# Where softmax row sums lie in DRAM: one attention kernel, two layouts

## Chip, cores and metric

The kernel runs on one core of a Trainium2 chip. The metric is the device time of one execution in microseconds (us); for several runs the median is given. The engines are named as in the profile: PE (TensorE, matmuls), PEld (its weight loads), DVE (VectorE), ACT (ScalarE), POOL (GpSimd), SP (SyncE, which here only issues transfers; its queue is SPq).

## What is computed

A transformer block with conditioning: attention over a window of a key and value cache, then a gated MLP. Cut to the part that the change touches (32 query heads on 16 key/value heads, 2048 queries, a window of 512 keys, head size 128):

```python
q = (x @ wq).reshape(B, Sq, Hq, Dh).transpose(0, 2, 1, 3)
k = jnp.repeat(k_cache[:, :, Sk - W:, :], rep, axis=1)
v = jnp.repeat(v_cache[:, :, Sk - W:, :], rep, axis=1)
scores = jnp.einsum("bhqd,bhkd->bhqk", q, k) * (Dh ** -0.5)
p = softmax(scores, axis=-1)
o = jnp.einsum("bhqk,bhkd->bhqd", p, v)
return o.transpose(0, 2, 1, 3).reshape(B, Sq, Hq * Dh) @ wo
```

Before it come a layer norm with shift and gain, and behind it a gate and the sum with x; then a second layer norm, `silu(h @ w1) * (h @ w3) @ w2`, a gate and a sum.

## The kernel before

The 2048 queries are cut into 4 blocks of SB = 512, and each block into ST = 4 tiles of P = 128. One head of one block is a slot; there are n = 128 slots, in an order written out by hand. f32 operands are split into a high and a low f16 part, so that a product is three matmuls.

Slot i has four steps, t = 0 to 3. In each, PE makes the scores of one tile (L395), DVE takes their maximum (L399, L400), and ACT takes the exponential p (L412) with the sum of each row beside it, in column t of a small tile l of 128 partitions. The work of neighbouring slots is laid between. Of slot i - 1, p is transposed by PE (L435), copied as the high part by ACT (L436), and DVE subtracts for the low part (L458); for one tile of four a DMA transpose on SPq does it (L451). At the end of slot i PE forms the unnormalized output po of slot i - 1, which has head dimension by queries (L468).

The sums of the rows lie one query per partition, but po has its queries along the free dimension. So they are turned by way of DRAM, in `sums` (slot i - 1, called in slot i): at step 0 the reciprocal of the four sums of each partition (L419), at step 1 the store of 128 x 4 values into a DRAM tile row (L422), and at step 2 the load of those 512 values into every partition, as tile r (L425). Both transfers are issued by SP, whose queue takes all other loads and stores of the stage in order too; L425 waits there until the data of L422 have landed, and L451 follows behind it.

In slot i, step 2, between the maximum of the third tile and the exponential of it, DVE multiplies po of slot i - 2 by r (`normalize`, L477) to give on. At step 3 `split_on` makes its high part on ACT (L487) and its low part on POOL (L488), and later PE multiplies with wo (L348) and DVE adds into acc (L496).

Row is stored as it lies in l: partition p, then t. Query t * 128 + p of the block is thus at place 4p + t of r, and L477 walks through r with `r.rearrange("d p t -> d t p")`.

From slot 16 on the same stage also makes the operands of the MLP ready: loads of w1, w3 and w2 (the tiles wraw and w2raw), sums and splits (wmade and omade), and stores of them (wd and od). The MLP itself (L757, L843) begins near the end of the attention stage; there DVE also has sums and products of the form f32 from PSUM with f32 from SBUF (L938, L944). L310 transposes keys; hp at L446 is the input of the DMA transpose. The load of the conditioning vector c into the tile sc at the very start (L98) takes its values one by one from DRAM, four to a partition.

Of the kernel before, what the change touches and what calls it, by code (L numbers as in the profile page):

```python
# [9 lines left out]
F32 = mybir.dt.float32  # L10
# [9 lines left out]
P = 128  # L20
# [4 lines left out]
SB = 512  # L25
NSB = S // SB
ST = SB // P
# [19 lines left out]
def tile_block(  # L47
# [14 lines left out]
    nc = tc.nc  # L62
# [4 lines left out]
    pool = ctx.enter_context(tc.tile_pool(name="pool", bufs=2))  # L67
    odd = ctx.enter_context(tc.tile_pool(name="odd", bufs=2))
    psum = ctx.enter_context(tc.tile_pool(name="psum", bufs=2, space=PSUM))
    dram = ctx.enter_context(tc.tile_pool(name="dram", bufs=1, space=DRAM))  # L70
# [344 lines left out]
    def sums(i, step):  # L415

        st = state[i]
        if step == 0:
            nc.vector.reciprocal(st["l"][:, ST:], st["l"][:, :ST])  # L419
        elif step == 1:  # L420
            st["row"] = dram.tile([P, ST], F32, name=f"row{i}")
            nc.sync.dma_start(st["row"], st["l"][:, ST:])  # L422
        elif step == 2:
            st["r"] = pool.tile([P, P, ST], F32, tag="kv", name="r", bufs=8)
            nc.sync.dma_start(  # L425
                st["r"].rearrange("d p t -> d (p t)"), st["row"].rearrange("p t -> (p t)").partition_broadcast(P)
            )

    def turn(i, t):

# [42 lines left out]
    def normalize(i):  # L473
        st = state[i]
        po = st.pop("po")
        on = st["on"] = pool.tile([P, SB], F32, tag="raw", name="on", bufs=RB)
        nc.vector.tensor_mul(  # L477
            on.rearrange("d (t p) -> d t p", t=ST),
            po.rearrange("d (t p) -> d t p", t=ST),
            st["r"].rearrange("d p t -> d t p"),  # L480
        )

    def split_on(i):
        st = state[i]
# [809 lines left out]
    for c in range(3):  # L1294
        i = 117 + 3 * c
# [107 lines left out]
    for i in range(n + 2):  # L1403
        run(i, -1)
        for t in range(ST):
# [9 lines left out]
            if 2 <= i <= n and t == 2:  # L1415
                normalize(i - 2)
# [8 lines left out]
            if 1 <= i <= n and t < 2:  # L1425
                sums(i - 1, t)
# [12 lines left out]
            if 1 <= i <= n and t == 2:  # L1439
                sums(i - 1, t)  # L1440
# [3 lines left out]
        if i == n:  # L1444
            normalize(n - 1)
            split_on(n - 1)
# [30 lines left out]
```

## Time and profile before

| | |
|---|---|
| median of 3 runs | 2908.57 us (2904.57 to 2909.78) |
| the profiled execution | 2906.05 us |
| its span | 2904.1 us |
| granted PE clock, mean | 0.995 |
| instructions | 47894 |
| DMA packets, bytes | 416049, 396.33 MB |

The span is the time from the first to the last instruction in the profile. Busy time of an engine is the time in which it worked on an instruction; matmuls overlap, so a busy PE is not PE at its peak. A wait is put down to the instruction that released it. Of a transfer, the profile gives the time from its issue to its landing.

### The profile page before, as it was taken

The page shows a single profiled execution, that of the slowest core. Times are in us where ns is not written, and L with a number is a line of the kernel's source. Part 1 is how long each engine was busy: PE and PEld are TensorE (multiplying, and loading weights), DVE is VectorE, ACT ScalarE, POOL GpSimd, SP SyncE. Part 2 cuts the span into 40 slices and gives each one's busy share as a digit, 9 for nine tenths or more (in the row PEclk, how much of TensorE's full clock was granted, in tenths as well). Part 3 has the DMA queues.
Part 4 walks back from the last instruction along what each step waited for, and adds up shares of the span by engine and source line. Part 5 has one row for each costly group of instructions (what it writes and reads, how often), then busy time and mean ns, then how long its engine had stood idle before and what let it go on. Part 6 is the DMA issues. An engine that isn't in the chain of part 4 may idle for free.

```text
span 2904.1 us, 47894 instructions
## 1 busy us (share of the span) xinstructions
PE 2832.3 (98%) x16624; PEld 1664.3 (57%) x16624; DVE 2104.7 (72%) x3762; ACT 1603.7 (55%) x3168; POOL 1668.0 (57%) x1796
## 2 busy tenths in 40 slices
PE   6999999999999999999999999999999999999998
PEld 3555556565655565555656555555555555555555
DVE  7777788888888888888786665666666665665656
ACT  4676777777777777787755662333333333323332
POOL 3344787778778777888722543445555455343345
PEclk9999999999999999999999999999999999999999
DMA  5535655665556577776734662444343443333332
GB/s 147 135 94 149 154 148 139 151 149 144 140 136 156 133 157 192 184 196 180 183 77 109 156 182 82 128 131 142 121 133 113 156 125 113 117 113 103 106 107 78
DMA packets 416049, 396.33 MB, mean 136 GB/s; under 512 B 180928, under 2 KB 302912, under 8 KB 415040
## 3 DMA queue, kind: packets, MB, share of 16 engines
q1 hardware_dynamic: 415200, 393.28, 49.8%
q8 instruction: 131, 2.15, 0.3%
q14 instruction: 110, 0.90, 0.1%
q10 hardware_dynamic: 608, 0.00, 0.0%
HBM read 263.60 MB, written 95.99 MB: 124 GB/s over the span
## 4 chain that ended last, share of the span: by engine, by line
PE 49%; DVE 2%; POOL 2%; issue 1%; ACT 1%; DMA 1%; SPq 0%; POOLq 0%; DVEq 0%; ACTq 0%
PE py L757 15%; PE px L757 11%; PE pe L843 6%; PE pf L843 6%; PE pe L348 3%; PE po L468 2%; PE pss L395 2%; PE pq L337 2%; PE pt L435 1%; DVE table L399 0%; PE pq L341 0%; DVE acc L496 0%; POOL omade L701 0%; DMA oraw<-in_A_wo 0%; DVE on L477 0%
## 5 line engine op out<-in xcount | busy, mean ns | idle before, releaser
L412 ACT ACTIVATE p<-pss,table,factors 128x512 f32<-128x512 f32 x512 | 399.0, 779 | 399.8 <-DVE table L400 329.4
L757 PEld LDWEIGHTS <-wset 128*128 128x128 f16 x3528 | 345.4, 98 | 337.0 <-issue 1.1
L757 PE MATMUL py<-hset,wset 128*128 128x512 f16 x2016 | 482.7, 379 | 0.0
L348 PE MATMUL pe<-o 128*128 128x288 f16 x3072 | 460.1, 287 | 5.8 <-DVE acc L496 5.8
L399 DVE TENSOR_REDUCE table<-pss 128x1 f32<-128x512 f32 x512 | 350.0, 684 | 133.9 <-PE pss L395 129.1
L395 PE MATMUL pss<-k,qT 128*128 128x512 f16 x1536 | 418.8, 381 | 2.5 <-ACT p L412 1.2
L348 PEld LDWEIGHTS <-o 128*128 128x128 f16 x3072 | 301.1, 98 | 176.8 <-issue 7.4
L468 PE MATMUL po<-ptw,v 128*128 128x512 f16 x1536 | 357.1, 380 | 6.1 <-DVE on L477 3.7
L757 PE MATMUL px<-hset,wset 128*128 128x512 f16 x1512 | 361.6, 379 | 0.0
L458 DVE TENSOR_TENSOR ptw<-pt,ptw 128x512 f16<-128x512 f32 x384 | 263.0, 685 | 62.3 <-ACT ptw L436 59.6
L93 POOL TENSOR_TENSOR akv<-u,akv 128x512 f16<-128x512 f32 x141 | 164.4, 1175 | 218.1 <-ACT akv L92 216.1
L488 POOL TENSOR_TENSOR o<-on,o 128x512 f16<-128x512 f32 x128 | 148.5, 1160 | 241.7 <-ACT o L487 219.6
L337 PE MATMUL pq<-hT,wq 128*128 128x512 f16 x1092 | 282.7, 381 | 1.6 <-DVE hT L205 1.6
L496 DVE SCALAR_TENSOR_TENSOR acc<-pe,factors,acc 128x576 f32<-128x576 f32 x256 | 208.0, 812 | 96.3 <-PE pe L348 76.4
L436 ACT CAST ptw<-pt 128x512 f16<-128x512 f32 x384 | 224.7, 585 | 69.2 <-PE pt L435 67.6
L435 PE MATMUL pt<-ident,p 128*128 128x128 f32 x1536 | 233.4, 275 | 15.8 <-ACT p L412 9.3
L468 PEld LDWEIGHTS <-v 128*128 128x128 f16 x1536 | 149.3, 99 | 169.0 <-issue 11.2
L843 PEld LDWEIGHTS <-akv 128*128 128x128 f16 x1728 | 169.1, 98 | 89.3 <-issue 0.8
L435 PEld LDWEIGHTS pt<-ident,p 128*128 128x128 f32 x1536 | 187.2, 143 | 52.5 <-ACT p L412 14.3
L662 POOL TENSOR_TENSOR wmade<-wraw,wmade 128x256 f16<-128x256 f32 x252 | 172.4, 684 | 53.7 <-ACT wmade L661 34.4
L395 PEld LDWEIGHTS <-qT 128*128 128x128 f16 x1536 | 150.5, 98 | 78.7 <-DVE qT L385 3.7
L337 PEld LDWEIGHTS <-wq 128*128 128x128 f16 x1104 | 109.0, 99 | 138.2 <-issue 8.3
(224 smaller groups left out, 4871.9 us busy)
## 6 DMA issues: line engine op xcount, KB each, us to landing
wset<-wd SPq DMA_DIRECT2D x213, 320.0 KB, 3.3
wd<-wmade SPq DMA_DIRECT2D x108, 320.0 KB, 3.7
r<-row SPq DMA_DIRECT2D x128, 256.0 KB, 4.2
oset<-od SPq DMA_DIRECT2D x106, 288.0 KB, 2.8
wraw<-in_B_w SPq DMA_DIRECT2D x144, 128.0 KB, 3.5
od<-omade SPq DMA_DIRECT2D x57, 288.0 KB, 3.8
wset<-wd SPq DMA_DIRECT2D x71, 160.0 KB, 2.3
w2raw<-in_B_w SPq DMA_DIRECT2D x38, 288.0 KB, 3.5
```

The source lines that it names most:

```text
L337: nc.tensor.matmul(ps, w[:, k // 2, m, :], hT[:, DC + m if k == 1 else m, :], start=s == 0, stop=False)
L348: nc.tensor.matmul(E[:, h, :HALF], o[:, x, rows], w[:, y, h * HALF : (h + 1) * HALF], start=first and n == 0, stop=last and n == 2,)
L395: nc.tensor.matmul(pss, q[:, x, rows], k[:, y, :], start=n == 0, stop=n == 2)
L399: nc.vector.tensor_reduce(nm[:, 0:1], pss, axis=AX.X, op=ALU.max, negate=True)
L412: nc.scalar.activation(p, pss, AF.Exp, bias=nm[:, 1:2], scale=factor, accum_out=st["l"][:, t : t + 1])
L435: nc.tensor.transpose(ps[:, j, :], p[:, j * P : (j + 1) * P], ident)
L436: nc.scalar.copy(st["pt"][:, 0, :, t * P : (t + 1) * P], st["t"])
L458: nc.vector.tensor_sub(pt[:, 1, :, cols], state[i]["t"], pt[:, 0, :, cols])
L468: nc.tensor.matmul(po, v[:, x, c, :], pt[:, y, c, :], start=c == 0 and n == 0, stop=c == KC - 1 and n == 2)
L496: nc.vector.scalar_tensor_tensor(a, E[:, :, :HALF], factors[:, uses[u][0], 2:3], a, op0=ALU.mult, op1=ALU.add)
L757: nc.tensor.matmul(ps, w[:, a, :], h[:, b, :], start=start and n == 0, stop=stop and n == 6, skip_group_check=True)
L843: nc.tensor.matmul(ps[:, h, :HALF], a[:, rows], w[:, b, :], start=m == 0, stop=m == 2)
```

## The change

The DRAM tile row has the shape 4 x 128 in place of 128 x 4, and the store writes it through a transposed view, so that query t * 128 + p lies at place 128t + p. The load copies 512 contiguous values to each partition as before, and r is a plain tile of 128 x 512. The multiplication takes po and r as they lie.

```diff
         elif step == 1:
-            st["row"] = dram.tile([P, ST], F32, name=f"row{i}")
-            nc.sync.dma_start(st["row"], st["l"][:, ST:])
+            st["row"] = dram.tile([ST, P], F32, name=f"row{i}")
+            nc.sync.dma_start(st["row"].rearrange("t p -> p t"), st["l"][:, ST:])
         elif step == 2:
-            st["r"] = pool.tile([P, P, ST], F32, tag="kv", name="r", bufs=8)
-            nc.sync.dma_start(
-                st["r"].rearrange("d p t -> d (p t)"), st["row"].rearrange("p t -> (p t)").partition_broadcast(P)
-            )
+            st["r"] = pool.tile([P, SB], F32, tag="kv", name="r", bufs=8)
+            nc.sync.dma_start(st["r"], st["row"].rearrange("t p -> (t p)").partition_broadcast(P))
...
         on = st["on"] = pool.tile([P, SB], F32, tag="raw", name="on", bufs=RB)
-        nc.vector.tensor_mul(
-            on.rearrange("d (t p) -> d t p", t=ST),
-            po.rearrange("d (t p) -> d t p", t=ST),
-            st["r"].rearrange("d p t -> d t p"),
-        )
+        nc.vector.tensor_mul(on, po, st["r"])
```

## Prediction

> **What bounds the kernel now.** I read the page first, then the busy times stretch by stretch, because the change touches only the attention stage, whose normalizations run from 85.7 to 1754.9 us.
>
> ```profile
> span 2904.1 us, 47894 instructions
> PE 2832.3 (98%) x16624; PEld 1664.3 (57%) x16624; DVE 2104.7 (72%) x3762; ACT 1603.7 (55%) x3168; POOL 1668.0 (57%) x1796
> ...
> core 0: us, PE busy (x) PEld busy (x) DVE busy (x) ACT busy (x) POOL busy (x), PEclk, DMA share, GB/s
> 60.00:500.00 440.00, 427.43 (x2520) 255.80 (x2518) 351.08 (x721) 311.49 (x633) 253.48 (x296) 0.99 0.53 135
> 500.00:1000.00 500.00, 493.76 (x2970) 297.91 (x2968) 414.17 (x830) 376.20 (x793) 387.09 (x484) 1.00 0.58 144
> 1000.00:1400.00 400.00, 390.79 (x2339) 234.06 (x2338) 340.84 (x691) 305.83 (x639) 329.02 (x398) 1.00 0.71 180
> 1400.00:1500.00 100.00, 96.51 (x583) 58.10 (x582) 75.41 (x159) 59.72 (x129) 47.94 (x54) 0.98 0.54 136
> 1500.00:1740.00 240.00, 237.47 (x1420) 142.59 (x1419) 166.24 (x321) 147.08 (x295) 93.18 (x85) 1.00 0.54 138
> ```
>
> TensorE (PE) is the bound in every stretch. VectorE (DVE), the next one, is at 80 to 85% until 1400 us. From 60 to 1740 us PE is idle for 12.6 + 6.2 + 9.2 + 3.5 + 2.5 = 34 us of 1680. That is the first fence around any gain: work taken from VectorE can only give back the part of these 34 us that VectorE causes. The waits of PE and of its weight loads (PEld) in the stretch 60 to 1740 us say which part that is. Columns: waiting engine and line, what it waited for, us in total, times, longest.
>
> ```profile
> PE pt L435 <- ACT p L412: 9.3, 10, 1.7
> PE po L468 <- DVE on L477: 3.7, 7, 1.2
> PE pt L435 <- DVE ptw L458: 2.8, 4, 0.8
> PE pt L310 <- DVE ptw L458: 1.5, 3, 0.6
> ...
> PEld pt L435 <- ACT p L412: 14.3, 15, 2.1
> PEld L468 <- DVE on L477: 5.5, 9, 1.5
> ```
>
> The instruction that changes, L477, is itself the releaser for 3.7 us on PE. The low parts of the transposed probabilities (L458), which stand behind it on VectorE, account for another 4.3 us.
>
> **The normalization itself.** Its rows, and those of the other products and sums of one operand in PSUM and one in SBUF with 512 columns of f32 out:
>
> ```profile
> L477 DVE TENSOR_TENSOR on<-po,r 128x512 f32<-128x512 f32 x128 | 139.3, 1088 | 2.1 <-PE po L468 1.8 <-issue 0.2
> L938 DVE TENSOR_TENSOR u<-px,u 128x512 f32<-128x512 f32 x72 | 49.8, 692 | 93.2 <-ACT u L937 93.2
> L944 DVE TENSOR_TENSOR u<-px,u 128x512 f32<-128x512 f32 x72 | 49.3, 685 | 0.7 <-PE px L757 0.7
> ```
>
> L477 takes 1088 ns, and the same form with both operands contiguous takes 685 to 692. The only difference that the code shows is the walk through r: element (p, t) lies at 4p + t, so successive elements are 16 bytes apart. After the change r is read in order, so I put the new time at 688 ns. The saving is 400 ns a head block, times 128 = 51.2 us of VectorE (2104.7 to about 2053.5). Most of it falls where PE does not wait and is worth nothing. What counts is where L477 stands just ahead of a release. The last of these places in the timeline:
>
> ```profile
> 1572.83 1.07 DVE L477 TENSOR_TENSOR on<-po,r 128x512 f32<-128x512 f32 x1
> ...
> 1573.83 0.68 DVE L458 TENSOR_TENSOR ptw<-pt,ptw 128x512 f16<-128x512 f32 x1
> ...
> 1574.65 0.63 PE L435 MATMUL pt<-ident,p 128*128 128x128 f32 x4 [0.68 <-DVE ptw L458]
> ```
>
> The low part starts when the normalization ends, and PE stands for 0.68 us until it is done; 0.4 us of that goes. The sum over such places:
> - L468 waiting for L477: 7 times, mean 0.53 us, so 7 x 0.40 = 2.8 us.
> - L435 and L310 waiting for L458: 7 times, 4.3 us. I take 5 of them as standing behind a normalization like the one above: 2.0 us.
> - L435 waiting for p: ScalarE waits there for a maximum that VectorE delivers. L477 lies between the maxima of the third and the fourth tile, so I count about a quarter of PEld's 15 waits: 4 x 0.40 = 1.6 us.
> - The end of the stage has one normalization in an unbroken row of VectorE work that PE waits for, the one of the next fence: 0.4 us.
>
> ```profile
> 1739.15 1.06 DVE L477 TENSOR_TENSOR on<-po,r 128x512 f32<-128x512 f32 x1
> ...
> 1743.42 2.74 PE L348 MATMUL pe<-o 128*128 128x288 f16 x12 [2.28 <-DVE acc L496]
> ```
>
> Together 6.8 us. What is late next in such a slot is PE itself, so I let the gain stand. The upper end of the gain takes PEld's 5.5 us, all 4.3 us and half of the 9.3 us: 14.5 us.
>
> **The store.** L422 wrote 16 bytes from each of 128 partitions in one piece. It now writes four single f32 from each, 512 bytes apart in DRAM: 512 pieces where there were 128. The read L425 stays 128 pieces of 2048 bytes. SyncE's queue (SPq) runs in order: L425 waits there for L422's data, and behind L425 are the DMA transpose of the low probabilities (L451) and the loads and stores of that step. No 4-byte write to DRAM is in the trace, so the bounds come from these rows (KB of one, median us from issue to landing):
>
> ```profile
> r<-row SPq DMA_DIRECT2D x128, 256.0 KB, 4.2
> wraw<-in_A_wq SPq DMA_DIRECT2D x32, 256.0 KB, 4.6
> row<-l SPq DMA_DIRECT2D x128, 2.0 KB, 1.9
> ...
> DMA to landing us min/median/max: 1.4/1.9/8.1
> ...
> q10 hardware_dynamic: 608, 0.00, 3.3%
> ...
> sc<-in_c ACTq DMA_DIRECT2D x1, 2.0 KB, 3.9
> ```
>
> The load of a wq column block moves the same 256 KB as r, in 512 pieces instead of 128, and lands 0.4 us later. That is the lower end; a gain is excluded, since there are only more pieces. The load of c into sc is 512 pieces of 4 bytes, though in the other direction and at the very start; it landed after 3.9 us, 2.0 over the row's 1.9. I take 1.0 us, nearer to the pair of equal bytes because sc's load also met a cold start. The far end is the longest landing of a row so far, 8.1 us, which is 6.2 more. The transfer itself is small: in the first 10 us the 608 pieces of q10 took 3.3% of 16 engines, 5.3 us or 8.7 ns each, so 512 of them are 0.28 us on each of 16 engines per slot, where the busiest stretch has a DMA share of 0.71.
>
> What covers 1 us on SPq is its own waiting:
>
> ```profile
> SPq L422 <- DVE l L419: 366.5, 81, 17.1
> ...
> SPq L451 <- POOL wmade L663: 154.3, 40, 7.0
> ...
> SPq L425 <- DMA row<-l: 96.3, 66, 6.8
> ...
> SPq L451 <- POOL hp L446: 51.2, 21, 12.8
> ```
>
> SPq already waits for the row 66 times. But it then also waits at L451 for the data of the transpose (154.3 + 51.2 us) and at the next L422 for the next reciprocal (366.5 us): 572 us over 128 slots, 4.5 us a slot. A row that lands 1 us later moves L425 in about half of the slots, and what follows hardly at all. The reader of r has time as well: the last r is issued at 1736.0 us and lands within 6.7, and its normalization runs at 1754.9.
>
> ```profile
> L425 SPq DMA_DIRECT2D r<-row x128: 318/328/1223, 61.9 to 1736.0; - x128
> L477 DVE TENSOR_TENSOR on<-po,r x128: 1041/1090/1133, 85.7 to 1754.9; 128x512 f32<-128x512 f32 x128
> ...
> DMA to landing us min/median/max: 3.1/4.2/6.7
> ...
> ACT p L412 <- DMA wraw<-in_B_w: 6.2, 3, 2.3
> ...
> DVE ptw L458 <- DMA ptw<-hp: 2.0, 1, 2.0
> ```
>
> Where a transfer is late today (the last two rows, four times), it may get up to 1 us later. I charge 0.8 us for all four.
>
> The Trainium skill, DMA: Bandwidth & Descriptors, section Rules for kernel authors, speaks against the change: a last dimension that is not contiguous becomes one descriptor per element and should be rearranged away. By that rule the count is my 512; the sum is the same unless each piece is dear, which is the second rival.
>
> **Sum.** 6.8 - 0.8 = 6.0 us. The profiled execution took 2906.05 us, 1.95 of them outside the span, and goes to 2900.05. It lies 2.5 us under the median of 2908.57, on which I forecast 2902.6.
>
> **The rivals.**
> *PE runs on as before.* The released time is given back: PE reaches its next wait 0.4 us sooner and waits there for something else (a transfer, GpSimd, ScalarE). For it: PE's own idle is 34 us of 1680, and most of its releasers are ScalarE. Against it: the rows above name VectorE directly. With the charge of 0.8 and no gain: 2909.4.
>
> *The row lands so late that SPq becomes the bound.* Place: L425 waiting for L422, with L451 and all loads behind it. It decides from a landing of 1.9 + 4.5 = 6.4 us on, where the waits that cover it are used up; from there each us costs 128 us. At 7.0 us it is 0.6 x 128 = 77 us, a time of about 2986. Below that point, at 5 us, only the slots with little slack are hit; if the four late transfers grow by 3 us each, that is 12 us less the gain: 2915. For it: neighbouring partitions write 4 bytes each into the same few bytes of DRAM, which nothing in the trace does, and rows have landed as late as 8.1 us. Against it: 512 pieces of 4 bytes landed in 3.9 us at the start, and 512 pieces in 4.6 us while carrying 256 KB.
> The Trainium skill, VectorE: DVE Perf Modes, section The three transpose paths, calls a plain DMA that transposes by strides 19 times slower than the DMA transpose when the destination's stride is large. If that factor fell on the row's 1.9 us, an estimate from that page would be 36 us, far over the point from which SPq decides; sc's 3.9 us disagrees, though its writes went to SBUF and no run here shows such a write to DRAM.
>
> *L477 stays near 1088 ns*, because something else than the walk through r makes it slow. Against it: L938 and L944 have the same form. Time 2909.4, as in the first rival.
>
> **How the numbers follow.** 0.62 for the forecast, 0.19 for PE running on, 0.16 for the late row, 0.03 for an unchanged L477. About 0.2% (5.8 us) is what a measurement of this kernel can tell from no change, and the forecast's 6.0 lies just beyond it: of its 0.62, I put 0.47 over the bound and 0.15 under. Faster 0.47; within 0.2% 0.15 + 0.19 + 0.03 = 0.37; slower 0.16. The forecast's own range is 2894 (the gain of 14.5 us) to 2905. The range over all cases reaches from 2894 to 2915, over the no-gain case and up to the mild form of the late row; it leaves out the rest of that case.
>
> **What would show it.** L477's mean: near 688 ns if the walk was the cost, 1088 if not. DVE busy: 51 us less. The wait of L468 for L477: from 3.7 us to under 1. The median landing of row<-l: 2.3 to 3.9 us if the pairing holds, over 6.4 if SPq decides; then the wait at L425 grows from 96 us to several hundred and the one at L422 shrinks. PE's idle from 60 to 1740 us: about 28 us instead of 34 if I am right, 34 if PE runs on as before. The forecast is wrong if L477 is at 688 ns and PE's idle stays, or if any PE wait names a transfer that it did not name before.

## The result, and the profile after

The changed kernel takes 3469.81 us (median of 4 runs, 3460.3 to 3475.13) against 2907.16 us before (now the median of 4 runs as well): a ratio of 1.194, with a 95% interval of 1.192 to 1.197. The forecast was 2902.6 us. The second rival came true, and dearer than it was priced.

The page of the changed kernel, its span, busy times and the chain that ended last. In the changed kernel the lines behind `normalize` have moved up: L466 is the old L468 (po), L475 the old L477 (the normalization), L449 the old L451 (the DMA transpose).

```profile
span 3473.1 us, 47895 instructions
...
PE 2989.7 (86%) x16624; PEld 1711.1 (49%) x16624; DVE 2063.3 (59%) x3762; ACT 1610.1 (46%) x3168; POOL 1668.2 (48%) x1796
...
PE 39%; DMA 19%; POOL 4%; SPq 3%; DVE 3%; issue 3%; ACT 1%; POOLq 0%; DVEq 0%; ACTq 0%
PE py L751 12%; PE px L751 9%; DMA row<-l 7%; PE pf L837 5%; PE pe L837 5%; DMA wd<-wmade 3%; PE po L466 2%; DMA w2raw<-in_B_w 2%; DMA r<-row 2%; DMA ptw<-hp 1%; PE pe L348 1%; PE pq L337 1%; PE pss L395 1%; DMA wraw<-in_B_w 1%; SPq L449 1%
```

PE is no longer the bound: its idle time has gone from 71.8 us (2904.1 - 2832.3) to 483.4 us (3473.1 - 2989.7), and its busy time has grown by 157.4 us for the same 16624 matmuls. The two make up the whole difference of the spans, 569 us. Transfers now hold 19% of the chain, the row ahead of all of them.

The waits of SyncE's queue, of VectorE and of PE (columns as in the prediction), and the normalization's group:

```profile
SPq L425 <- DMA row<-l: 966.4, 96, 15.0
...
SPq L422 <- DVE l L419: 47.0, 9, 14.4
...
DVE on L475 <- DMA r<-row: 313.0, 77, 9.6
...
PE po L466 <- DMA ptw<-hp: 199.2, 53, 8.2
PE pe L1052 <- DVE table L1047: 114.8, 16, 19.7
...
L475 DVE TENSOR_TENSOR on<-po,r 128x512 f32<-128x512 f32 x128 | 88.1, 688 | 332.6 <-DMA r<-row 313.0 <-POOL wmade L656 8.1 <-POOL w2raw L706 4.0
```

The normalization takes 688 ns, as forecast to the nanosecond. But SPq waits ten times as long for the row at L425 (966.4 us after 96.3), and it hardly waits any more for the next reciprocal at L422 (47.0 us after 366.5): the queue, which used to be ahead of VectorE, is behind it. So r is late for the normalization, the DMA transpose is late for po, and PE stands: PE's largest wait names a transfer that it did not name before, which the prediction had put down as a sign of being wrong. L1047 looks for the peak of w2raw, a load that has nothing to do with the row except that it stands behind it; VectorE's wait there grew from 0.3 to 143.1 us. VectorE's busy time fell by 41.4 us, where 51 was foretold: the normalization gave the 51.2, and other work on it took some 10 more.

SyncE's and VectorE's rows in the first slot, where only one other store (L322) lies between the store and the load, and in a later one:

```profile
59.36 0.17 DVE L419 RECIPROCAL l<-l 128x4 f32<-128x4 f32 x1
59.55 0.40 SPq L422 DMA_DIRECT2D row<-l  x1
60.01 0.49 SPq L322 DMA_DIRECT2D kept_k(0,)_643<-k  x1
68.79 0.33 SPq L425 DMA_DIRECT2D r<-row  x1
...
900.39 0.38 SPq L422 DMA_DIRECT2D row<-l  x1
...
903.54 10.18 SPq L640 DMA_DIRECT2D wraw<-in_B_w  x4
914.94 0.35 SPq L425 DMA_DIRECT2D r<-row  x1
...
SPq L640 <- DMA row<-l: 46.8, 7, 10.0
```

The first slot of the kernel before, which has the same store at L322 there:

```profile
60.46 0.36 SPq L422 DMA_DIRECT2D row<-l  x1
...
61.90 0.32 SPq L425 DMA_DIRECT2D r<-row  x1
```

From the store to the load that waits for it 9.2 us pass in the first slot and 14.5 us in the later one; before, it was 1.4 us in the first. The first slot is among the quickest of both kernels: over all 128 slots, read off the same rows, the median is 12.7 us (9.2 to 20.1), and 3.0 us before. The profile gives no landing times for the changed kernel, so this time stands in their place. In the later slot it is not all landing of the row: 8.4 us of it SPq stood at the small loads of L640, which the profile also puts down to the row (the last line of the first fence has these waits in all).

The busy share of the DMA engines from 59 to 69 us, in slices of 0.25 us, and their packets:

```profile
DMA  0000007989700000000000000000000000000000
DMA packets 673, 0.27 MB, mean 27 GB/s; under 512 B 544, under 2 KB 544, under 8 KB 672
```

The engines work for little more than 1 us. By 62 us they have taken 543 of the 544 packets under 512 bytes, among which are the row's 512; from 65.5 to 68.5 us they take none, and still SPq stands until 68.79. So most of the 9.2 us passes after the engines have taken the pieces, and before the store counts as landed.

### The profile page after: what moved, and what is told of

Same layout as the page of the kernel before. It is cut to its first block, busy times and chain, and to the rows that moved or that the text cites. A ratio compares the mean times of both kernels' runs of the same rounds, so it can differ in the third digit from the quotient of the medians.

```text
span 3473.1 us, 47895 instructions
## 1 busy us (share of the span) xinstructions
PE 2989.7 (86%) x16624; PEld 1711.1 (49%) x16624; DVE 2063.3 (59%) x3762; ACT 1610.1 (46%) x3168; POOL 1668.2 (48%) x1796
## 4 chain that ended last, share of the span: by engine, by line
PE 39%; DMA 19%; POOL 4%; SPq 3%; DVE 3%; issue 3%; ACT 1%; POOLq 0%; DVEq 0%; ACTq 0%
PE py L751 12%; PE px L751 9%; DMA row<-l 7%; PE pf L837 5%; PE pe L837 5%; DMA wd<-wmade 3%; PE po L466 2%; DMA w2raw<-in_B_w 2%; DMA r<-row 2%; DMA ptw<-hp 1%; PE pe L348 1%; PE pq L337 1%; PE pss L395 1%; DMA wraw<-in_B_w 1%; SPq L449 1%
## 5 line engine op out<-in xcount | busy, mean ns | idle before, releaser
L466 PE MATMUL po<-ptw,v 128*128 128x512 f16 x1536 | 472.5, 471 | 235.3 <-DMA ptw<-hp 199.2
L348 PE MATMUL pe<-o 128*128 128x288 f16 x3072 | 467.5, 290 | 14.6 <-DVE acc L490 14.6
L466 PEld LDWEIGHTS <-v 128*128 128x128 f16 x1536 | 172.8, 116 | 487.9 <-DVE on L475 226.8
L475 DVE TENSOR_TENSOR on<-po,r 128x512 f32<-128x512 f32 x128 | 88.1, 688 | 332.6 <-DMA r<-row 313.0
L433 PE MATMUL pt<-ident,p 128*128 128x128 f32 x1536 | 242.0, 282 | 10.6 <-ACT hf L207 6.4
L433 PEld LDWEIGHTS pt<-ident,p 128*128 128x128 f32 x1536 | 196.5, 149 | 52.8 <-issue 10.3
```

The costliest lines, as they stand in the source:

```text
L348: nc.tensor.matmul(E[:, h, :HALF], o[:, x, rows], w[:, y, h * HALF : (h + 1) * HALF], start=first and n == 0, stop=last and n == 2,)
L433: nc.tensor.transpose(ps[:, j, :], p[:, j * P : (j + 1) * P], ident)
L466: nc.tensor.matmul(po, v[:, x, c, :], pt[:, y, c, :], start=c == 0 and n == 0, stop=c == KC - 1 and n == 2)
```

## Experiments

**The two halves of the change, each alone.** First the walk, with the old store and load:

```diff
-            st["r"].rearrange("d p t -> d t p"),
+        nc.vector.tensor_mul(on, po, st["r"].rearrange("d p t -> d (p t)"))
```

> Only the walk is changed: store and load as in the kernel before, and the multiplication reads r as it lies (the reciprocals are then applied in the wrong order of queries; nothing is left out of the work). If the part of the prediction on VectorE was right: L477 at 688 ns, PE's idle from 60 to 1740 us down by about 7 us, time 2900 (6 to 7 us under the kernel before). If PE runs on as before: within 3 us of it.

2895.4 us (5 runs), ratio 0.9962 (0.9949 to 0.9976): 11 us under the kernel before. The waits of PE, the busy times, and the stretch from 60 to 1740 us:

```profile
PE pt L435 <- ACT p L412: 8.7, 9, 1.8
...
PE pt L435 <- DVE ptw L458: 1.6, 4, 0.6
...
PE 2826.4 (98%) x16624; PEld 1662.2 (57%) x16624; DVE 2055.4 (71%) x3762; ACT 1601.5 (55%) x3168; POOL 1665.0 (58%) x1796
...
L468 PE MATMUL po<-ptw,v 128*128 128x512 f16 x1524 | 353.9, 380 | 3.4 <-ACT ptw L436 1.0 <-DVE on L477 0.8
...
60.00:1740.00 1680.00, 1649.75 (x9857) 991.45 (x9856) 1301.55 (x2722) 1198.39 (x2485) 1111.25 (x1316) 1.00 0.59 150
L477 DVE TENSOR_TENSOR on<-po,r x128: 678/680/692, 84.2 to 1745.3; 128x512 f32<-128x512 f32 x128
```

The wait of L468 for the normalization fell from 3.7 to 0.8 us, the one of L435 for the low part from 2.8 to 1.6, and the one for p only from 9.3 to 8.7. The last normalization starts at 1745.3 us instead of 1754.9. PE runs on as before is refuted: the gain of the walk is real, and somewhat larger than the 6.8 us of the forecast's sum. But it does not all lie where the sum looked for it. PE's idle time from 60 to 1740 us is 30 us, where 34 stood before and 28 was foretold. Over the whole span (2904.1 us before, 2894.2 now) it fell by 4.0 us, from 71.8 to 67.8; the other 5.9 us are PE's busy time, for the same 16624 matmuls. Kernels with the old walk reach as little as 2825.0 us of it (the one with the second store into SBUF, below), so no run here says what that part is.

Then the store alone, with the old walk over r (an edit of the changed kernel):

> Only the store is changed: 4-byte pieces as in the changed kernel, the load as there, and the multiplication walks through r in steps of 16 bytes (in the wrong order of queries). If the store is the whole of the loss: 3465 to 3490, as the changed kernel or a little over it, with the multiplication at 1088 ns. If the shorter multiplication had a part in it (VectorE stands and waits at another place): clearly under 3465.

```diff
-        nc.vector.tensor_mul(on, po, st["r"])
+        nc.vector.tensor_mul(
+            on.rearrange("d (t p) -> d t p", t=ST),
+            po.rearrange("d (t p) -> d t p", t=ST),
+            st["r"].rearrange("d (p t) -> d t p", t=ST),
+        )
```

3427.21 us, ratio 1.180 (1.178 to 1.182), with SPq waiting 939.6 us at L425. The store is the loss. That it comes out 1.2% lower than the changed kernel, which has the shorter normalization as well, is the second branch of the expectation: beside this store the shorter instruction seems to cost time rather than to save it, but no run here says why.

**Is it the wait, or the transfers behind?** Here the kernel before keeps its own store and load, and issues the 4-byte store beside it, into a tile that nobody reads:

```diff
             nc.sync.dma_start(st["row"], st["l"][:, ST:])
+            side = st["side"] = dram.tile([ST, P], F32, name=f"side{i}").rearrange("t p -> p t")
+            nc.sync.dma_start(side, st["l"][:, ST:])
```

> The kernel before, with the 4-byte store as a second store beside its own, into a DRAM tile that nobody reads. Nothing waits for it. If only the wait of L425 for its own row costs the time: under 2930 (one more issue on SyncE's queue a slot). If the store holds up the transfers behind it on the DMA engines too: most of the 560 us, over 3200, with L425 waiting long for the ordinary row.

3320.66 us, ratio 1.143 (1.141 to 1.145). No instruction uses what it wrote, and it still costs 415 us. The waits and the stretch from 60 to 1740 us (L427 is the load of r here, L479 the normalization, L648 one of the loads of w1 and w3, L1055 the peak of w2raw):

```profile
SPq L427 <- DMA row<-l: 314.3, 71, 13.5
SPq L648 <- DMA side<-l: 58.6, 10, 9.2
...
DVE on L479 <- DMA r<-row: 179.5, 51, 10.3
DVE table L1055 <- DMA w2raw<-in_B_w: 117.2, 17, 14.5
...
60.00:1740.00 1680.00, 1390.53 (x7710) 804.84 (x7709) 1096.07 (x2205) 982.10 (x2031) 950.01 (x1154) 0.91 0.90 119
```

The other transfers are late: the old row, r, the loads of w2 (0.3 us of waiting for them at this place before). SPq itself also stands until the unread store has landed, at loads that use nothing of it (L648, and smaller waits at other lines); why it does so there, no run shows. The DMA engines show as busy for 0.90 of the stretch while they move only 119 GB/s; in the walk-alone kernel it was 0.59 at 150 GB/s.

With a load of 4 bytes from that tile in front of the load of r, the queue waits for the store in every slot:

```diff
         elif step == 2:
+            nc.sync.dma_start(st["l"][:1, :1], st["side"][:1, :1])
```

> As the one before, and a load of 4 bytes from that tile in front of L425, so that SyncE's queue waits for the 4-byte store as in the changed kernel. If the wait of the queue is what costs: about 3470, with some 9 to 14 us from the store to the load. If blocked transfers cost all: the same time as without the load, within 20 us.

3449.13 us, ratio 1.187 (1.185 to 1.190), so both theories hold a part. Of the excess of 0.187, the unread store alone makes 0.143 (three quarters) by what it does to the other transfers and to the queue, and the wait for it in every slot adds the rest. This kernel is the yardstick for the next ones, in which only the second store is another.

**What makes the store slow?** Each has the load of 4 bytes behind it. The edits, from the 512 adjacent pieces (row 1 of the table) on:

```diff
-            side = st["side"] = dram.tile([ST, P], F32, name=f"side{i}").rearrange("t p -> p t")
-            nc.sync.dma_start(side, st["l"][:, ST:])
+            side = st["side"] = dram.tile([1, P], F32, name=f"side{i}").rearrange("t p -> p t")  # one column, adjacent
+            side = st["side"] = dram.tile([P, 2], F32, name=f"side{i}")[:, :1]  # one column, 8 bytes apart
+            side = st["side"] = dram.tile([P, 4], F32, name=f"side{i}")[:, :1]  # one column, 16 bytes apart
+            nc.sync.dma_start(side, st["l"][:, ST : ST + 1])  # with each of these three
...
+            side = st["side"] = dram.tile([P, ST, 2], F32, name=f"side{i}")[:, :, 0]  # four columns, 8 bytes apart
+            side = st["side"] = dram.tile([P, ST, 16], F32, name=f"side{i}")[:, :, 0]  # four columns, 64 bytes apart
+            side = st["side"] = dram.tile([P, ST], F32, name=f"side{i}")  # pieces of 16 bytes, adjacent
+            nc.sync.dma_start(side, st["l"][:, ST:])  # with each of these three
```

> The control for the stores that follow: the second store is the one of the kernel before once more (128 pieces of 16 bytes, neighbours adjacent), with the load of 4 bytes behind it. Both theories: 2 us from the store to its landing, time 2905 to 2930; what is over the kernel before is the price of two more transfers and a second wait on SyncE's queue.

> The second store writes 512 pieces of 4 bytes, but each 64 bytes from the next, so that no two partitions write close together. If it is the number of small writes to DRAM that costs: like the transposed 4-byte store, 3400 to 3480, landing 9 to 14 us. If it is that neighbouring partitions write into the same few bytes and are served one after another: landing 2 to 4 us, time under 2950.

> The second store writes only the first of the four columns, 128 pieces of 4 bytes that lie side by side in one row of 512 bytes (three of four values of that unread tile are left out). As many pieces as the ordinary row. If the number costs: 2 to 3 us to land, time under 2950. If the closeness costs: the pieces share their bytes as closely as in the transposed store, so it lands nearly as late (8 us or more where the rows are served side by side, a quarter of the excess if they are served one after another) and the time is over 3050.

> One column as a second store again, 128 pieces of 4 bytes, but 16 bytes apart: as close as the 16-byte pieces of the ordinary row, with a quarter of the bytes. If what counts is how many pieces fall into the same few bytes: like the ordinary row, under 2930. If pieces under 16 bytes are slow at any distance below 64 bytes: over 3100.

> The same, 8 bytes apart. If the time to land follows the number of pieces that share a stretch of DRAM: between the two, landing about half of the 9.5 us of the adjacent pieces, time between 2930 and 3150. If there is a bound between 4 and 16 bytes under which everything is slow: as the adjacent pieces, near 3260, or as the ones 16 bytes apart.

> 512 pieces of 4 bytes, 8 bytes apart, four of them from the same partition and then the next partition's. Four times as many pieces as in the one-column store with this distance. If what counts is how many pieces share a stretch, from whatever partition: like that store, or slower. If pieces of one partition do not disturb each other: clearly faster than it, under 2950.

| second store | pieces | median us | ratio (95%) | first slot, store to load, us | wait at L426, us in all |
|---|---|---|---|---|---|
| 4 bytes, transposed: neighbours adjacent | 512 | 3449.13 | 1.187 (1.185 to 1.190) | 11.2 | 802.3 |
| 4 bytes, one column, adjacent | 128 | 3261.6 | 1.123 (1.117 to 1.129) | 9.5 | 760.7 |
| 4 bytes, one column, 8 apart | 128 | 2915.32 | 1.005 (1.004 to 1.007) | 4.5 | 261.2 |
| 4 bytes, one column, 16 apart | 128 | 2905.8 | 1.001 (1.000 to 1.002) | 3.7 | 116.5 |
| 4 bytes, 8 apart | 512 | 2940.06 | 1.013 (1.010 to 1.015) | 5.3 | 327.6 |
| 4 bytes, 64 apart | 512 | 2908.47 | 1.002 (1.001 to 1.003) | 3.9 | 193.8 |
| 16 bytes, adjacent (the control) | 128 | 2905.42 | 1.001 (1.000 to 1.002) | 3.9 | 108.6 |

The last two columns are read from rows like these, the store and the load behind it in the first slot of four of the kernels (transposed; one column adjacent; four columns 64 bytes apart; control), and the wait of the load at L426:

```profile
60.44 0.43 SPq L424 DMA_DIRECT2D side<-l  x1
...
71.59 0.30 SPq L426 DMA_DIRECT2D l<-side  x1
...
SPq L426 <- DMA side<-l: 802.3, 87, 12.6
```

```profile
59.45 0.42 SPq L424 DMA_DIRECT2D side<-l  x1
...
68.94 0.30 SPq L426 DMA_DIRECT2D l<-side  x1
...
SPq L426 <- DMA side<-l: 760.7, 97, 11.4
```

```profile
58.83 0.61 SPq L424 DMA_DIRECT2D side<-l  x1
...
62.77 0.29 SPq L426 DMA_DIRECT2D l<-side  x1
...
SPq L426 <- DMA side<-l: 193.8, 84, 6.2
```

```profile
60.62 0.42 SPq L424 DMA_DIRECT2D side<-l  x1
...
64.56 0.30 SPq L426 DMA_DIRECT2D l<-side  x1
...
SPq L426 <- DMA side<-l: 108.6, 71, 5.4
```

The control lands after 3.9 us where I expected 2: the ordinary row and another store stand beside it in the queue, so only differences between the rows of the table count. Over all 128 slots the median times from store to load are, in the order of the table, 11.5, 10.1, 4.5, 3.2, 5.3, 4.0 and 3.1 us, so the first slot gives much the same order.

The number of pieces is not what costs: 512 of them, 64 bytes apart, land 0.9 us after the control (4.0 and 3.1 us) and add 0.2%, and 128 adjacent ones add 12%. The size is not, either: 4 bytes at 16 bytes' distance do as well as 16 bytes. What costs is that pieces of 4 bytes lie side by side in DRAM. It falls off fast with distance: 9.5 us in the first slot when adjacent, 4.5 at 8 bytes, 3.7 at 16, about the control's time. In proportion to the pieces that share a stretch, 8 bytes would give half of 9.5; the landing agrees with that, but the time (2915) is far below the 2930 that I expected at least. SPq's wait for the next reciprocal, which shrank from 329.1 us in the control to 241.6, covers part of it.

By the medians, lying 8 bytes apart costs 1.3 us for one column (4.5 after 3.2 us at 16 bytes) and 1.3 us for four (5.3 after 4.0 at 64 bytes), although the four have pieces of the same partition as neighbours: these count like those of other partitions. Being adjacent costs 7.0 us for 128 pieces and 7.5 us for 512.

One rival stays. The closer the pieces lie, the smaller are the multiples of bytes on which they start, so alignment changes along with closeness. A price for each badly aligned piece, paid one after another, would be four times as much for 512 pieces as for 128, and it is not. But no run has pieces far apart that start off a 16-byte boundary.

One more separates DRAM from SBUF: 512 pieces of 4 bytes, 16 bytes apart, into the tile r.

```diff
+            st["r"] = pool.tile([P, P, ST], F32, tag="kv", name="r", bufs=8)
+            side = st["r"][:, :ST, 0]
+            nc.sync.dma_start(side, st["l"][:, ST:])
```

> The second store is again 512 pieces of 4 bytes, 16 bytes apart, but into SBUF (into the tile r, which the load of L425 overwrites after it, so L425 waits for it). If writing to DRAM is what makes 4-byte pieces slow: landing 2 to 3 us, time under 2930. If 512 pieces of 4 bytes are slow wherever they go: over 3300.

2903.47 us, ratio 1.000 (0.999 to 1.001). In the first slot the load of r follows 3.7 us after this store (58.67 to 62.38 us), as in the control. Many 4-byte pieces into SBUF cost nothing. They are 16 bytes apart, so this does not say what adjacent pieces would do there.

**A version without the adjacent pieces.** VectorE turns the reciprocals in blocks of 32 x 32, so that the store writes 128 bytes from each partition and the normalization reads runs of 32:

```diff
         if step == 0:
-            nc.vector.reciprocal(st["l"][:, ST:], st["l"][:, :ST])
+            r = st["r"] = pool.tile([P, SB], F32, tag="kv", name="r", bufs=8)
+            nc.vector.reciprocal(
+                r[:, :32].rearrange("p (a t) -> p a t", t=ST),
+                st["l"][:, :ST].rearrange("p (a t) -> p a t", a=1).broadcast_to([P, 8, ST]),
+            )
+            nc.vector.transpose(r[:, 32:64], r[:, :32])
         elif step == 1:
-            st["row"] = dram.tile([P, ST], F32, name=f"row{i}")
-            nc.sync.dma_start(st["row"], st["l"][:, ST:])
+            st["row"] = dram.tile([P, 32], F32, name=f"row{i}")
+            nc.sync.dma_start(st["row"], st["r"][:, 32:64])
         elif step == 2:
...
+            row = st["row"].rearrange("(q c) j -> q c j", q=ST)[:, :ST].rearrange("q c j -> q (c j)")
+            nc.sync.dma_start(
+                st["r"].rearrange("d (q n) -> d q n", q=ST), row.partition_broadcast(P)
+            )
...
-            st["r"].rearrange("d p t -> d t p"),
+            st["r"].rearrange("d (q t j) -> d t q j", q=ST, t=ST),
```

> A version meant to keep the shorter multiplication without the 4-byte store: VectorE writes the reciprocals eight times side by side (32 columns), turns blocks of 32 x 32, the store writes 128 pieces of 128 bytes, the load takes 512 pieces of 512 bytes, and the multiplication reads runs of 32 values. If closeness of small pieces was the whole loss and the walk the whole gain: the multiplication at about 690 ns, some 150 to 200 ns a slot for the turn and the longer reciprocal, time 5 to 10 us under the kernel before (2895 to 2900). If transfers on the way cost more than that: at or over the kernel before.

2899.55 us, ratio 0.9989 (0.9980 to 0.9998): about 0.1% under the kernel before, just clear of the noise, and far under the changed one. Its groups on VectorE, and SPq's wait for its row:

```profile
L482 DVE TENSOR_TENSOR on<-po,r 128x512 f32<-128x512 f32 x128 | 87.2, 681 | 2.5 <-PE po L473 1.8 <-issue 0.7
L420 DVE RECIPROCAL r<-l 128x32 f32<-128x32 f32 x128 | 43.9, 343 | 0.0
L424 DVE STREAM_TRANSPOSE r<-r 128x32 f32<-128x32 f32 x128 | 27.1, 211 | 4.4
...
SPq L430 <- DMA row<-r: 85.3, 64, 6.2
```

The multiplication has the short time and the row lands as it did before (85.3 us of waiting after 96.3). But the longer reciprocal (343 ns after 167) and the turn (211) give 387 of the 407 ns back. VectorE's work is nearly the same in sum, so what is left of the gain should come from where that work stands; no run separates this. The load of r, now 512 pieces of 512 bytes, lands after 5.5 us (median) where it took 4.2. The gain is 4.5 us, just under the 5 to 10 that I expected.

## Why the prediction was wrong

- *What bounds the kernel, and the normalization.* Right in the mechanism. PE was the bound, the walk was the whole extra cost of the multiplication (688 ns after 1088, VectorE's group 88.1 us after 139.3, the forecast 51.2 us), and the walk alone gives a gain: 11 us where I had summed 6.8 and put 14.5 as the upper end. The terms of L468 and of the low parts went as argued (3.7 to 0.8 and 2.8 to 1.6 us); the term of p did not (9.3 to 8.7, where 1.6 was counted). That the measured gain is near the sum is in part luck: PE's waiting accounts for 4.0 of the 9.9 us between the two traces, and where the rest comes from stays open.
- *The store.* This is the step that failed. I put 1.0 us on its later landing, between 0.4 and 2.0, with 6.2 as the far end. From store to load it was 7.8 us more in the first slot (9.2 against 1.4), and 9.7 by the medians of all slots (12.7 against 3.0). I took the lower end from two loads into SBUF that differ in the number of pieces, and the upper from 512 pieces of 4 bytes that also went to SBUF. So all rows that I compared were about number and size, and for number the 1.0 us was a good estimate: 512 pieces of 4 bytes, 64 bytes apart in DRAM, land 0.9 us after the control and add 0.2%. No row of the trace had pieces of 4 bytes side by side in DRAM, and that was what counted. I had written it down as the argument for the second rival and then sized the step by the rows that lacked it.
- *What covers it on SPq.* The form was right: the wait at L425 grew to several hundred us (966.4) and the one at L422 shrank (366.5 to 47.0), as the text said for a landing over 6.4 us. At 128 us for each us over 6.4, the mean of all slots (12.9 us) would give about 830 us; it was 563. So the price was not too low: the rival was cheap because it was worked out for 7.0 us. But the rule counts SPq's own wait alone. The store that nobody reads shows what was missing: the transfers that follow it land late as well, and that alone is 415 us. The cover for r (issued a slot ahead of its reader) is gone for the same reason, since r is issued late and lands late: 313.0 us of waiting at the normalization, where the trace of before has none.
- *The chances.* 0.16 on the late row was too little for a step whose far end lay at the point from which SPq decides, and for which no row was of the same kind. The range ended at 2915 because I left the rest of that case out.
- *The two rules cited.* The Trainium skill, DMA: Bandwidth & Descriptors, Rules for kernel authors, warns of one descriptor per element. The advice was right here, but the number of descriptors is not the reason. The factor of 19 in the Trainium skill, VectorE: DVE Perf Modes, The three transpose paths, compares such a copy with the DMA transpose. The estimate of 36 us put it on an ordinary store instead, which the page does not say; 9.2 us after 1.4 is a factor of 6.6. The row that I set against it wrote to SBUF.

## What to carry to other kernels

When a store changes its layout in DRAM, ask not only how many pieces it has and how long they are, but how close to each other they land: a transposed store of f32 puts words from neighbouring partitions side by side. Transpose on an engine before the store instead, so that each piece is long, and weigh what that engine pays (387 of 407 ns here). And where a bound rests on rows that lack the very property that is new, keep the far end in the range.

## What was not expected of the hardware

- Writes of 4 bytes side by side in DRAM: 128 of them took 9.5 us to land, and 128 pieces of 4 bytes at 16 bytes' distance 3.7 us, about as much as 128 adjacent pieces of 16 bytes (3.9 us). The runs fit a price for pieces that share a stretch (or, not separated, for their alignment), not for short pieces as such. The Trainium skill, DMA: Bandwidth & Descriptors, Specifications, says that pieces under 512 bytes are read, modified and written. In the first slot the time passes after the DMA engines have taken the pieces; where in the path they queue up then, and how wide the stretch is, no run here shows.
- Such a store delays transfers that have nothing to do with it. Beside the unread one, VectorE waits up to 14.5 us for loads of w2, and in the later slot above four small loads behind the row took SPq from 903.54 to 913.72 us.
- PE loses twice. Besides the waits, its matmuls are slower, as these stretches of the changed kernel, its group of L466 and the same group before (L468) show:

```profile
500.00:1000.00 500.00, 397.87 (x2191) 230.80 (x2191) 298.90 (x620) 281.03 (x588) 287.56 (x359) 0.88 0.64 104
...
2400.00:3473.00 1073.00, 1063.40 (x6170) 604.25 (x6168) 660.99 (x861) 350.26 (x597) 507.31 (x430) 1.00 0.38 119
L466 PE MATMUL po<-ptw,v 128*128 128x512 f16 x1536 | 472.5, 471 | 235.3 <-DMA ptw<-hp 199.2
...
L468 PE MATMUL po<-ptw,v 128*128 128x512 f16 x1536 | 357.1, 380 | 6.1 <-DVE on L477 3.7
```

The granted clock is 0.88 in this stretch of the attention stage, where it was 1.00 before, and 1.00 in the MLP; the matmuls of po have a mean of 471 ns, where they had 380. That group alone accounts for 115 of the 157 us by which PE's busy time grew. The Trainium skill, TensorE: Matmul & The Clock Gate, Part 1, describes a clock that is lowered after an idle stretch of some 3.4 us. Waits of up to 8.2 us at L466 and a clock of 0.88 agree with it.
